# The start addresses of a part of TensorE's operands, moved by 32 to 224 bytes modulo 256

## The chip, the cores and the metric

The kernel runs on one core of one Trainium2 chip. The metric is the device time of one execution in microseconds. The kernel before the change takes 1422.89 us (median of 3 runs, 1422.87 to 1423.13).

## The reference: what is computed

Two kinds of layer alternate, A, B, A, B, each added to its input, on x of 2048 rows (the sequence) by 512 columns in float32:

```python
x = x + _A_ref(_layernorm(x), seq_re, seq_im, hid_re, hid_im)   # a Fourier mixing layer
x = x + _B_ref(_layernorm(x), w1, w2, w3, w4)                   # spatial shift, then an MLP
...                                                             # both once more
```

Layer A is Re(DFT_seq(DFT_hid(x))): two products of x with 512 x 512 matrices and two with 2048 x 2048 matrices. Layer B normalizes, multiplies by w1 (512 x 512), applies gelu, shifts each quarter of the columns by one or two rows up or down, multiplies by w2, adds, normalizes again, multiplies by w3 (512 x 1376), applies gelu, multiplies by w4 (1376 x 512) and adds.

## The kernel before, in words

**Three matmuls for one product.** Every operand of TensorE is split in a high half (rounded to the fp32r format) and a low half (what the rounding left). `mm3` (lines 293 to 296) multiplies high x high (L294), high x low (L295) and low x high (L296) into the same PSUM bank. So nearly every line of the profile for TensorE is L294, L295 or L296, and which product it is shows only in the names of its tiles. A matmul has 128 x 128 weights (the stationary operand, `lh` or `ll`) and a moving operand of 512 columns, or 256 in `first_pair`. There are 6441 of them, beside 12 in float32 on `ident` at the start (L139), which the profile counts as 24. The profile names a matmul's operands as out<-moving,weights.

**Where tiles lie.** One tensor, "arena", holds nearly the whole of SBUF. The tiles lie at hand-written places in it, counted in words of 4 bytes (`at`, `both`; lines 80 to 130), and tiles of different stages share the same places. Sizes and bases are nearly all multiples of 64 words = 256 bytes. So all tiles of TensorE start at one and the same address modulo 256 bytes, except those at and after STG, which starts 32 words past such a multiple: `w11` and one of the two h11 tiles, and the high halves `hr2` to `hr7`, are 128 bytes off the others. Slices of a tile that a matmul reads start at multiples of 128 words within it.

**The stages**, twice (once per layer pair):

- Layer A: `plain_phase` (for the first column block of the first layer), `x_phase` and `y_phase` for each of four blocks of 512 sequence columns. Moving operands are the DFT blocks in the four `ring` tiles: `stream()` hands out the next one, slots 0 to 3 in rotation, each filled by a DMA into a `raw` tile and a split by ACT (L240) and DVE (L257). Weights are the normalized rows and their sums and differences: `ax` (8 tiles, in `x_phase`), `ay` (8 tiles, in `y_phase`; 4 or 2 products per ring tile). Between them `hid` multiplies by the 512 x 512 matrices, with `rr` as weights and ring tiles as moving operand.
- Layer B, first half: `by_pairs` with `shifted` (moving `zt`, two tiles in turn; weights w1) and `mixed` (moving w2; weights `rg`), 16 of each per layer, interleaved.
- Layer B, second half: `prod` (weights `w3b`, moving the blocks `b11` to `b22` and `bt1` to `bt4`, seven products in place of eight, in the manner of Strassen) and `w4_part` (weights `h4`, moving `w4r`, loaded in turn into six or four slots). The last layer has its own code for it: `first_pair` (256 columns; weights `hr` for the high half and `hn` for the low half, moving `un`) and `last_pair` (weights `u1`, `u2` and `w11`).

**What orders the work.** The order is written out by hand; each engine works through its instructions in program order, and semaphores tie them. Hooks (`hook(i)`, `one()`, `at_point`, the slot lists `A` and `D` in `by_pairs`) put the work of ACT, DVE and the DMA queue between the matmuls of TensorE. All DMAs are issued from SyncE's queue. The change touches none of this.

**Names and lines that matter for the change**: `ZW`, `RNG`, `EXT`, `RAWS`, `STG`, `TMP` (lines 70 to 82, the bases of regions: EXT follows the ring and is followed by RAWS, STG and TMP); `ay_at` (L92), `zt` (L95), `turned0` (L99), `ring` (L105), the list of `bt` places (L112), `w4_at` (L119), `w4_in` (L1652), `w4_sum` (L1667).

Of the kernel before, what the change touches and what calls it, by code (L numbers as in the profile page):

```python
# [8 lines left out]
F32 = mybir.dt.float32  # L9
# [4 lines left out]
P = 128  # L14
S, D, F = 2048, 512, 1376
# [4 lines left out]
CH = 512  # L20
NC = S // CH
TC = CH // P
KD = D // P
DH = D // 2
NF = -(-F // P)
# [8 lines left out]
RING = 4  # L34
# [9 lines left out]
def spectral_mlp_kernel(ctx: ExitStack, tc: tile.TileContext, x, ws, hs, w1, w2, w34, out):  # L44
# [26 lines left out]
    ZW = KD * 2 * CH + 32  # L71
    AX, AY = 3 * 2 * DH, 4 * 2 * DH
    W12, XS = 2 * ZW, 2 * ZW + 8 * 2 * CH
    H3 = XS + NT * D
    SPARE = H3 + (LAG + 1) * 2 * CH
    RR = SPARE + 2 * D
    RNG = RR + 2 * KD * 2 * CH
    base = -(-nc.sbuf_base // 32) * 32
    EXT = RNG + RING * 4 * CH
    RAWS = EXT + 6 * D  # L80
    STG = RAWS + RAW * 2 * CH + 32
    TMP = STG + 2 * CH
# [2 lines left out]
    def at(name, word, *shape, dtype=F32R):  # L85
        return nc.alloc_sbuf_tensor_at(name, [P, *shape], dtype, offset=base + 4 * word).ap()

    def both(name, word, *shape):
        return at(name, word, *shape), at(name + "f", word, *shape, dtype=F32)

    tmp = at("tmp", TMP, 6, D, dtype=F32)
    ay_at = (0, AY, H3, H3 + AY, EXT, 2 * AY, 3 * AY, 4 * AY)  # L92
    ay, ayf = zip(*(both(f"ay{k}", ay_at[k], 4, 2, DH) for k in range(NP)))
    ax, axf = zip(*(both(f"ax{k}", XS - 8 * D + k * AX, 3, 2, DH) for k in range(NP)))
    zt, ztf = zip(*(both(f"zt{i}", i * (ZW + 32), KD, 2, CH) for i in range(2)))  # L95
    w12 = [at(f"w12{i}", W12 + i * 4 * CH, 2, 2, CH) for i in range(4)]
    beside = at("beside", XS - 4 * D - 32, 4, D, dtype=F32)
    xs = [at(f"xs{i}", XS + i * 2 * D, 2, D, dtype=F32) for i in range(NP)]
    turned0 = at("turned0", 5 * AY, KD, CH, dtype=F32)  # L99
    turned01 = at("turned01", H3, KD, CH, dtype=F32)  # L100
    spare = at("spare", SPARE, 2, D, dtype=F32)
    (re0, im0), (re1, im1) = ([both(f"rr{i}{h}", RR + (2 * i + h) * 4 * CH, 2, 2, CH) for i in range(2)] for h in range(2))
    rr = [[re0[0], re1[0]], [im0[0], im1[0]]]
    rg = [[at(f"rg{i}{g}", RR + (4 * i + g) * 2 * CH, 2, CH) for g in range(KD)] for i in range(2)]
    ring, ringf = zip(*(both(f"ring{i}", RNG + i * 4 * CH, 2, 2, CH) for i in range(RING)))  # L105
    raw_at = [at(f"raw{i}", RAWS + i * 2 * CH, 2, CH, dtype=F32) for i in range(RAW)]
    raw_at += [at(f"raw{RAW + i}", word, 2, CH, dtype=F32) for i, word in enumerate((EXT + 4 * D, STG))]

    blk, blkf = {}, {}
    for i, word in (("11", H3), ("21", H3 + 4 * CH), ("12", RNG), ("22", RNG + 4 * CH)):  # L110
        blk[i], blkf[i] = both("b" + i, word, 2, 2, CH)
    for i, word in enumerate((0, 4 * CH, RR, RR + 4 * CH)):  # L112
        blk[f"t{i + 1}"], blkf[f"t{i + 1}"] = both(f"bt{i + 1}", word, 2, 2, CH)
    w3b, w3bf = zip(*(both(f"w3b{i}", RNG + 8 * CH + i * 28 * P, 2, 7, 2 * P) for i in range(2)))
    h4 = [at(f"h4{i}", RR + 8 * CH + i * 2 * CH, 2, CH) for i in range(4)]
    hc = at("hc", W12, NF, CH, dtype=F32)
    staged = at("staged", STG, 2, 2, 2 * P, dtype=F32)
    hx = at("hx", STG, 2, CH, dtype=F32)
    w4_at = [2 * ZW + (i - 4) * 2 * CH for i in range(4)] + [W12 + NF * CH + i * 2 * CH for i in range(2)]  # L119
    w4r, w4rf = zip(*(both(f"w4r{i}", word, 2, CH) for i, word in enumerate(w4_at)))  # L120
    scratch = [at(f"scr{i}", RNG + w * 4 * CH, KD, CH, dtype=F32) for i, w in enumerate((2, 3, 0))]
    extra = [at(f"extra{i}", EXT + i * D, D, dtype=F32) for i in range(6)]
    gt = [at(f"gt{g}", RAWS + 4 * D + g * GW, CH + HALO, dtype=F32) for g in range(KD)]
# [1525 lines left out]


    w4_from = [(w34[NF - 1][:, 0], w3e)] + [(w34[f + LAG][:, 1], w4d[f]) for f in range(NF)]
    w4_in = [both(f"w4in{i}", word, 2, CH) for i, word in enumerate((5 * AY, 5 * AY + 2 * CH, STG, EXT + 4 * D))]  # L1652

    def w4_split(i):
        for n in (i - 5, i - 4, i - 3):
# [8 lines left out]
                    nc.sync.dma_start(wf[:, 1], w4_from[n][0])  # L1664

    w4_raw = at("w4raw", STG, 2, CH, dtype=F32)
    w4_sum, w4_sumf = both("w4sum", 5 * AY, 4, 2, 2 * P)  # L1667
    W4_AT = {(0, 2): 0, (0, 3): 1, (1, 1): 2, (1, 2): 3, (1, 3): 4}

    def w4_bring(k):  # L1670
# [261 lines left out]
```

## Time and profile before

| | before |
|---|---|
| median of 3 runs | 1422.89 us |
| the profiled execution | 1423.03 us |
| its span, first to last instruction | 1421.1 us |
| matmul records, weight load records | 6465, 6465 |
| bytes moved by DMA | 306.31 MB |

The page's first part gives the time in which each engine had at least one instruction under way. For TensorE (PE) the matmuls are pipelined: the next one starts long before the last one's modelled end, so the busy time is no measure of how fast they follow each other. That is read from the starts of single matmuls in the timeline, or from the number of matmuls in a window. Busy digits are tenths of a slice of 35.5 us. "PEclk" is the clock that was granted to TensorE.

### The profile page before, as it was taken

How to read it: one execution, taken by the hardware profiler on the slowest of the kernel's cores; microseconds unless marked ns; L12 is line 12 of the kernel's file. 1: busy time of each engine (PE TensorE's matmuls, PEld its weight loads, DVE VectorE, ACT ScalarE, POOL GpSimd, SP SyncE). 2: the span in 40 equal slices, each digit the busy share in tenths (PEclk: the TensorE clock that was granted, in tenths of full speed). 3: DMA queues.
4: the chain of work that ended last, by engine and by line, in shares of the span. 5: the costliest groups of instructions: out<-in, count | busy, mean ns of one | idle time of the engine just before them, and what ended most of it. 6: DMA issues, size and time to landing. Idle time of an engine off the chain costs nothing.

```text
span 1421.1 us, 17861 instructions
## 1 busy us (share of the span) xinstructions
PE 1415.4 (100%) x6465; PEld 1180.1 (83%) x6465; DVE 1187.0 (84%) x1675; ACT 743.0 (52%) x1007; POOL 77.7 (5%) x105
## 2 busy tenths in 40 slices
PE   9999999999999999999999999999999999999998
PEld 7888888888888888888888888888888888899887
DVE  7986998988979888656789989889899788896676
ACT  6663464455566754434555544554555566453351
POOL 2100000000002000000000000000000020000000
PEclk9999999999999999999999999999999999999999
DMA  7867647659754857945556476575696456676864
GB/s 253 279 208 234 210 152 262 193 163 309 238 164 109 294 195 266 354 159 178 196 174 222 152 253 212 158 265 176 193 304 229 134 148 237 202 244 228 311 207 158
DMA packets 136488, 306.31 MB, mean 216 GB/s; under 512 B 9680, under 2 KB 58064, under 8 KB 133712
## 3 DMA queue, kind: packets, MB, share of 16 engines
q1 hardware_dynamic: 136400, 305.17, 65.1%
q8 instruction: 51, 0.84, 0.2%
q14 instruction: 37, 0.30, 0.1%
HBM read 250.87 MB, written 54.26 MB: 215 GB/s over the span
## 4 chain that ended last, share of the span: by engine, by line
PE 93%; DVE 4%; ACT 1%; issue 1%; POOL 0%; DMA 0%; DVEq 0%; ACTq 0%; POOLq 0%
PE psd L294 10%; PE psd L296 10%; PE psd L295 9%; PE psa L296 8%; PE psa L294 8%; PE psa L295 8%; PE psb L296 7%; PE psc L295 7%; PE psc L296 7%; PE psb L294 7%; PE psb L295 7%; PE psc L294 7%; DVE rest L480 0%; ACT tmp L342 0%; DVE ring L257 0%
## 5 line engine op out<-in xcount | busy, mean ns | idle before, releaser
L240 ACT CAST ring<-raw 128x1024 fp32r<-128x1024 f32 x127 | 133.3, 1054 | 78.5 <-PE psd L296 42.9
L257 DVE TENSOR_TENSOR ring<-raw,ring 128x1024 fp32r<-128x1024 f32 x126 | 153.5, 1220 | 13.1 <-ACT ring L240 13.0
L294 PE MATMUL psd<-ring,rr 128*128 128x512 f32 x208 | 80.9, 389 | 0.0
L295 PE MATMUL psd<-ring,rr 128*128 128x512 f32 x208 | 80.9, 389 | 0.0
L296 PE MATMUL psd<-ring,rr 128*128 128x512 f32 x208 | 80.9, 389 | 0.0
L334 POOL TENSOR_TENSOR rs<-ve,mhalf 128x4 f32<-128x4 f32 x16 | 26.9, 1683 | 723.8 <-DVE nm L333 723.8
L247 ACT CAST ring<-ring0f 128x1024 fp32r<-128x1024 f32 x28 | 29.6, 1057 | 50.7 <-DVE ring0f L246 50.7
L257 DVE TENSOR_TENSOR ring<-ring1f,ring 128x512 fp32r<-128x512 f32 (+1 forms) x56 | 53.3, 952 | 0.7 <-ACT ring L243 0.7
L313 POOL TENSOR_TENSOR rs<-ve,mhalf 128x2 f32<-128x2 f32 (+2 forms) x33 | 28.8, 872 | 415.7 <-DVE nb L312 415.7
L342 ACT ACTIVATE tmp<-xs,nb,rs 128x512 f32<-128x512 f32 x56 | 43.5, 814 | 14.6 <-POOL nb L314 14.6
L294 PE MATMUL psc<-ring,ay 128*128 128x512 f32 x128 | 49.8, 389 | 0.0
L295 PE MATMUL psc<-ring,ay 128*128 128x512 f32 x128 | 49.8, 389 | 0.0
L296 PE MATMUL psc<-ring,ay 128*128 128x512 f32 x128 | 49.8, 389 | 0.0
L294 PE MATMUL psb<-ring,ay 128*128 128x512 f32 x128 | 49.8, 389 | 0.0
L295 PE MATMUL psb<-ring,ay 128*128 128x512 f32 x128 | 49.8, 389 | 0.0
L296 PE MATMUL psb<-ring,ay 128*128 128x512 f32 x128 | 49.8, 389 | 0.0
L294 PE MATMUL psa<-ring,ay 128*128 128x512 f32 x126 | 49.0, 389 | 0.0
L295 PE MATMUL psa<-ring,ay 128*128 128x512 f32 x126 | 49.0, 389 | 0.0
L296 PE MATMUL psa<-ring,ay 128*128 128x512 f32 x126 | 49.0, 389 | 0.0
L294 PE MATMUL psd<-ring,ay 128*128 128x512 f32 x126 | 49.0, 389 | 0.0
L295 PE MATMUL psd<-ring,ay 128*128 128x512 f32 x126 | 49.0, 389 | 0.0
L296 PE MATMUL psd<-ring,ay 128*128 128x512 f32 x126 | 49.0, 389 | 0.0
(826 smaller groups left out, 4494.4 us busy)
## 6 DMA issues: line engine op xcount, KB each, us to landing
raw<-in_ws SPq DMA_DIRECT2D x183, 512.0 KB, 5.1
raw<-in_hs SPq DMA_DIRECT2D x56, 512.0 KB, 3.6
w4r<-w4d SPq DMA_DIRECT2D x44, 512.0 KB, 4.5
w3b<-w3d SPq DMA_DIRECT2D x10, 1792.0 KB, 8.9
w3d<-w3b SPq DMA_DIRECT2D x5, 1792.0 KB, 6.9
x1d<-tmp SPq DMA_DIRECT2D x12, 512.0 KB, 6.4
xs<-x1d SPq DMA_DIRECT2D x12, 512.0 KB, 5.0
w4d<-w4in SPq DMA_DIRECT2D x11, 512.0 KB, 4.7
```

Source lines behind the costliest of these rows:

```text
L240: nc.scalar.copy(dest[:, a:b, 0], r[0][:, a:b])
L247: nc.scalar.copy(dest[:, :, 0], lo)
L257: nc.vector.tensor_tensor(lo, src, hi.bitcast(F32), op=ALU.subtract)
L294: nc.tensor.matmul(o, lh, rh, start=first, stop=False, skip_group_check=more)
L295: nc.tensor.matmul(o, lh, rl, start=False, stop=False, skip_group_check=more)
L296: nc.tensor.matmul(o, ll, rh, start=False, stop=last, skip_group_check=more)
L313: nc.gpsimd.tensor_tensor(rs[:, :n], ve[:, :n], mhalf[:, 0, :n], op=ALU.pow)
L334: nc.gpsimd.tensor_tensor(rs, ve, mhalf[:, :, :2], op=ALU.pow)
L342: nc.scalar.activation(o, s, AF.Identity, bias=mr[2], scale=mr[1])
```

## The change

The base of the region EXT moves up by 8 words (32 bytes), and with it everything behind it: RAWS, STG and TMP. Beside this some tiles get offsets of their own. No instruction is added or left out, and the order of the instructions is as before. In words modulo 64 (256 bytes), counted from the level that most tiles keep:

- ring: slots 0 to 2 stay at 0, slot 3 goes to 8
- ay: 0 to 3 stay at 0, ay4 goes to 8 (it lies at EXT), ay5 to 8, ay6 to 16, ay7 to 24
- zt: zt0 to 24, zt1 to 48
- bt: bt1 to 8, bt2 to 40, bt3 and bt4 stay at 0
- w4r: slots 0 to 3 to 56 (8 words lower), slots 4 and 5 stay at 0
- by the shift of EXT: hr0 and hr1, one of the h11 tiles of `first_pair`, both of `last_pair` and a few hn and hs tiles to 8; w11, hr2 to hr7 and the other h11 of `first_pair` from 32 to 40
- ax, rr, rg, w12 (w1 and w2), w3b, h4, b11 to b22, un, u1 and u2 stay at 0
- turned0, w4in and w4sum, which TensorE does not read, move by 24 words with ay7

```diff
-    EXT = RNG + RING * 4 * CH
+    EXT = RNG + RING * 4 * CH + 8
...
-    ay_at = (0, AY, H3, H3 + AY, EXT, 2 * AY, 3 * AY, 4 * AY)
+    ay_at = (0, AY, H3, H3 + AY, EXT, 2 * AY + 8, 3 * AY + 16, 4 * AY + 24)
...
-    zt, ztf = zip(*(both(f"zt{i}", i * (ZW + 32), KD, 2, CH) for i in range(2)))
+    zt, ztf = zip(*(both(f"zt{i}", word, KD, 2, CH) for i, word in enumerate((24, ZW + 16))))
...
-    turned0 = at("turned0", 5 * AY, KD, CH, dtype=F32)
+    turned0 = at("turned0", 5 * AY + 24, KD, CH, dtype=F32)
...
-    ring, ringf = zip(*(both(f"ring{i}", RNG + i * 4 * CH, 2, 2, CH) for i in range(RING)))
+    ring, ringf = zip(*(both(f"ring{i}", RNG + i * 4 * CH + word, 2, 2, CH) for i, word in enumerate((0, 0, 0, 8))))
...
-    for i, word in enumerate((0, 4 * CH, RR, RR + 4 * CH)):
+    for i, word in enumerate((8, 4 * CH + 40, RR, RR + 4 * CH)):
         blk[f"t{i + 1}"], blkf[f"t{i + 1}"] = both(f"bt{i + 1}", word, 2, 2, CH)
...
-    w4_at = [2 * ZW + (i - 4) * 2 * CH for i in range(4)] + [W12 + NF * CH + i * 2 * CH for i in range(2)]
+    w4_at = [2 * ZW + (i - 4) * 2 * CH - 8 for i in range(4)] + [W12 + NF * CH + i * 2 * CH for i in range(2)]
...
-    w4_in = [both(f"w4in{i}", word, 2, CH) for i, word in enumerate((5 * AY, 5 * AY + 2 * CH, STG, EXT + 4 * D))]
+    w4_in = [both(f"w4in{i}", word, 2, CH) for i, word in enumerate((5 * AY + 24, 5 * AY + 24 + 2 * CH, STG, EXT + 4 * D))]
...
-    w4_sum, w4_sumf = both("w4sum", 5 * AY, 4, 2, 2 * P)
+    w4_sum, w4_sumf = both("w4sum", 5 * AY + 24, 4, 2, 2 * P)
```

## The prediction

> Two words are used throughout. A matmul's **distance** is the start address of its weights minus that of its moving operand, modulo 256 bytes; at distance zero the two are **level**, otherwise **apart**. About 0.2% (3 us) is what a measurement of this kernel can tell from no change.
>
> **What bounds the kernel now.** I read the page first, then the waits of TensorE, then its share of a long stretch, then single starts.
>
> ```profile
> PE 1415.4 (100%) x6465; PEld 1180.1 (83%) x6465; DVE 1187.0 (84%) x1675; ACT 743.0 (52%) x1007; POOL 77.7 (5%) x105
> ...
> PEclk9999999999999999999999999999999999999999
> ...
> q1 hardware_dynamic: 136400, 305.17, 65.1%
> ```
>
> PE is busy for the whole span and its clock is never reduced. Busy time of pipelined matmuls says little by itself, so the next view matters more: the waits of TensorE, all of them.
>
> ```profile
> PE psd L139 <- POOL mhalf L55: 1.4, 1, 1.4
> PE psb L426 <- DVE rr L339: 0.2, 1, 0.2
> ```
>
> After the first microseconds TensorE waits for nobody. So the time is the number of matmuls times the interval from one start to the next, and nothing that DVE, ACT or the DMA queue does ends last anywhere. The interval comes from the windows view (PE busy with its count, then the clock) and, more exactly, from the timeline, whose columns are start, duration, engine, line, and operands as out<-moving,weights:
>
> ```profile
> 100.00:1200.00 1100.00, 1099.89 (x4851) 1.00 0.64 212
> ```
>
> ```profile
> 399.71 0.39 PE L294 MATMUL psb<-ring,rr 128*128 128x512 f32 x1
> ...
> 401.97 0.39 PE L295 MATMUL psc<-ring,rr 128*128 128x512 f32 x1
> ```
>
> 1100 us over 4851 matmuls is 0.2268 us, and the ten intervals between the two quoted starts take 2.26 us. The 0.39 us is the pipelined latency of one and is not the price of one. I call 0.2267 us the **settled** interval: nearly all 512-column matmuls keep to it, whatever their tiles, and nearly all of those are level. Only a settled rhythm that can be lost, or bettered, can be moved by this change.
>
> **When the rhythm is lost.** Two places show it at distance zero: a matmul that has a semaphore wait in front of it shifts the start a little, and the following starts need some matmuls to find the rhythm again.
>
> ```profile
> 444.13 0.39 PE L295 MATMUL psd<-w,rg 128*128 128x512 f32 x1
> ...
> 445.52 0.39 PE L295 MATMUL psd<-w,rg 128*128 128x512 f32 x1
> ```
>
> ```profile
> 465.92 0.39 PE L295 MATMUL psd<-w,rg 128*128 128x512 f32 x1
> ...
> 468.24 0.39 PE L296 MATMUL psd<-w,rg 128*128 128x512 f32 x1
> ```
>
> Six intervals take 1.39 us in place of 1.36, and ten take 2.32 in place of 2.267. One loss of the rhythm costs 0.03 to 0.053 us, and it heals after five to ten matmuls.
>
> **The nearest thing to the change in this trace.** The weights w11 of last_pair lie in the staging tile STG, which is 128 bytes off the rest (RAWS ends 32 words past a multiple). So six matmuls in a row are apart by 128, between level ones. The third to eighth rows are those six; the view calls them psa<-h,w.
>
> ```profile
> 1367.51 0.39 PE L295 MATMUL psd<-hs,u 128*128 128x512 f32 x1
> 1367.73 0.40 PE L296 MATMUL psd<-hia,u 128*128 128x512 f32 x1
> 1367.96 0.40 PE L294 MATMUL psa<-h,w 128*128 128x512 f32 x1
> 1368.21 0.40 PE L295 MATMUL psa<-h,w 128*128 128x512 f32 x1
> 1368.44 0.39 PE L296 MATMUL psa<-h,w 128*128 128x512 f32 x1
> 1368.67 0.39 PE L294 MATMUL psa<-h,w 128*128 128x512 f32 x1
> 1368.90 0.39 PE L295 MATMUL psa<-h,w 128*128 128x512 f32 x1
> 1369.13 0.40 PE L296 MATMUL psa<-h,w 128*128 128x512 f32 x1
> 1369.36 0.39 PE L294 MATMUL psa<-hia,u 128*128 128x512 f32 x1
> 1369.59 0.39 PE L295 MATMUL psa<-hs,u 128*128 128x512 f32 x1
> ```
>
> The weights of the next matmul are loaded while the present one streams, so the first interval concerned starts at 1367.73. From there to 1369.59 are eight intervals in 1.86 us; settled ones would take 1.813. Nothing here waits; only the distance changed, and it cost 0.047 us. The first six alone, up to 1369.13, take 1.40 in place of 1.36 us.
>
> The second sample points the other way. In first_pair the matmuls have 256 columns, and their weights, the high halves hr, are either level with the moving tile un (two of the eight hr tiles) or 128 apart (six of them):
>
> ```profile
> 1265.20 0.28 PE L294 MATMUL psd<-un,hr 128*128 128x256 f32 x1
> ...
> 1266.64 0.28 PE L294 MATMUL psb<-un,hr 128*128 128x256 f32 x1
> 1266.76 0.27 PE L295 MATMUL psb<-un,hr 128*128 128x256 f32 x1
> 1266.87 0.28 PE L296 MATMUL psb<-un,hn 128*128 128x256 f32 x1
> ...
> 1268.06 0.28 PE L294 MATMUL psd<-un,hr 128*128 128x256 f32 x1
> ```
>
> The level dozen takes 1.44 us (0.12 each), the dozen with its hr apart 1.42. Here the disturbed rhythm is the faster one, by 0.02 us in twelve, and the shortest single interval is 0.11 in place of 0.12.
>
> **The change part by part.** No instruction is added, removed or reordered; no DMA changes in size or place in the queue, and no wait is added. Only addresses move.
>
> 1. Tiles that TensorE doesn't read (raw, extra, staged and tmp by the shift of EXT; turned0, w4in and w4sum with ay7) move by 32 or 96 bytes. DVE, ACT and the DMA engines touch them, and I cost this at nothing: TensorE has no wait for any of them above, DVE is busy 84%, ACT 52%, the DMA engines 65%. If DVE's accesses became over a tenth slower the cover would be thin; nothing suggests that.
>
> 2. Matmuls that become apart. I walked the matmuls in program order with the diff's offsets. The groups view carries the classes (each line stands for one bank pair and one of the three products):
>
> ```profile
> L294 PE MATMUL psd<-ring,rr 128*128 128x512 f32 x208 | 80.9, 389 | 0.0
> L294 PE MATMUL psc<-ring,ay 128*128 128x512 f32 x128 | 49.8, 389 | 0.0
> L294 PE MATMUL psc<-ring,ax 128*128 128x512 f32 x112 | 43.6, 389 | 0.0
> L294 PE MATMUL psd<-zt,w 128*128 128x512 f32 x64 | 24.9, 389 | 0.0
> L294 PE MATMUL psa<-w4r,h 128*128 128x512 f32 x44 | 17.1, 389 | 0.0
> L294 PE MATMUL psb<-bt,w3b 128*128 128x512 f32 x40 | 15.6, 389 | 0.0
> ```
>
> Of 1536 ring,ay matmuls 864 become apart (ay4 to ay7 against an unmoved ring, and every fourth ring slot); of 960 ring,rr 384; of 1008 ring,ax 96; all 384 of zt,w (64 x 2 bank pairs x 3 products); 444 of 528 w4r,h and all 96 that use w4r as weights; 240 of 480 on bt with w3b; 28 others, 24 of them those of w11, which are apart already. That is 2536 of 512 columns. They come in 180 runs of constant distance (74 of 6, 62 of 12, 22 of 24, 13 of 36, nine others), with 144 level runs between them: 324 runs, each beginning with a change of distance. About nine of these exist already around w11, so 315 are new.
>
> 3. The price of one change of distance is not shown for 32 bytes, only for 128. Bounds: half the w11 excursion, which has two changes, 0.047 / 2 = 0.024 us; and one full loss of rhythm, 0.053 us. The nearest row is the first six intervals of w11: 1.40 against 1.36, 0.037 us before rounding of the starts. I take that: 315 x 0.037 = 11.7 us, with ends 7.4 and 16.7. All of it is on the path, because TensorE is never idle. Below nothing the price could go too, by the 256-column sample; that is a rival.
>
> 4. The 256-column matmuls: the two level hr tiles and hm1 become apart, some ten dozens at 0.02 us saved each: -0.2 us.
>
> A rule of the Trainium skill speaks against any effect. "SBUF — State Buffer", section "Who interferes with whom", has TensorE with two independent read ports, one for the moving operand and one for the weights, and waiting on no one; by it the sum would be zero. The w11 rows do not agree with it, since there only an address differs and 0.047 us appear.
>
> Sum against the profiled execution: 1423.03 + 11.7 - 0.2 = 1434.5 us; the span is 1421.1, with 1.9 us around it. The median of the runs is 1422.89, 0.14 lower, so **1434 us**. With the ends of step 3 the forecast's own range is 1430 to 1440.
>
> **The rivals.**
>
> *Faster: apart is the better state.* If the settled 0.2267 us holds a collision of the weight load with the moving stream, apart operands avoid it. For it: the 256-column dozens. Against it: w11, and every loss of rhythm above, cost time at 512 columns. Priced with 0.02 / 12 = 1.7 ns for each of the 2536: -4.2 us, 1418.6. Priced with the best single interval, 0.11 for 0.12 (112 against 120 ns before rounding): 2536 x 8 ns = -20.3 us, 1402.6. It decides if a run of 12 or more at constant distance settles below 0.2267; w11's six are too few to tell.
>
> The Trainium skill ("TensorE: Matmul & The Clock Gate", section "Wait — 56ns, not 53.3ns?") states 215.7 ns for back-to-back 512-column matmuls at full clock. The settled rows are 11 ns above; were all of that regained, an estimate by that page would be 2536 x 11 ns = 28 us.
>
> *Slower still: apart never settles.* Then each apart matmul pays w11's average, 0.037 / 6 = 6.2 ns: 2536 x 6.2 = 15.7 us, and each of the 144 level runs a loss of 0.03: 4.3. Together 1443.
>
> *No difference.* Distances of 32 to 96 bytes may be too small to matter, and w11's cost may belong to 128 alone: 1423. That the layout isn't what the title says can be excluded for the count above, which follows from the offsets; but half of the matmuls stay level, so a settled interval of 0.2267 will still be seen.
>
> **How the numbers follow.** Forecast (rhythm lost at each change and found again, 1430 to 1440) 0.44; never settles (1440 to 1446) 0.18; no difference 0.11; faster (1402 to 1419) 0.27. Slower by over 0.2% is therefore 0.62, within 0.2% 0.11, faster 0.27. A range that holds 8 in 10 must reach into the faster cases: 1409 to 1444 leaves out the far end of each.
>
> **What would show it.** Right: TensorE still without waits; level runs of rr, ax and rg at 0.2267; the first six intervals after each change of distance near 0.233; the apart count's price in the windows (442 matmuls per 100 us down to about 438). The forecast is wrong if zt,w or w4r,h, which hold one distance for 12 to 36 matmuls, run below 0.2267, if nothing differs, or if a wait of TensorE appears.

## The result and the profile after

The changed kernel takes **1442.3 us** (median of 4 runs, 1442.09 to 1442.33), the kernel before 1422.95 us beside it (4 runs, 1422.87 to 1423.13). The ratio is 1.0135, with a 95% interval of 1.0118 to 1.0153: slower by 19 us. The span of the profiled execution went from 1421.1 to 1440.1 us.

The changed kernel's page, its busy times, granted clock and DMA queue:

```profile
PE 1434.7 (100%) x6465; PEld 1179.9 (82%) x6465; DVE 1188.7 (83%) x1675; ACT 741.1 (51%) x1007; POOL 77.2 (5%) x105
...
PEclk9999999999999999999999999999999999999999
...
q1 hardware_dynamic: 136400, 305.17, 63.5%
```

The same counts of instructions and packets, the same bytes, the full clock. DVE, ACT and POOL are busy for the same time as before to within 2 us; PE's time alone has grown by about as much as the kernel's. The changed kernel's waits of TensorE are one line, the start of the kernel:

```profile
PE psd L139 <- POOL mhalf L55: 1.4, 1, 1.4
```

So no wait was added, and the 19 us must lie in the intervals between matmuls. The windows view of the changed kernel, for the stretch that was shown of before:

```profile
100.00:1200.00 1100.00, 1100.00 (x4778) 1.00 0.62 207
```

4778 matmuls where there were 4851: 0.2302 us each in place of 0.2268. The groups view shows a trace of it in the modelled duration of one matmul (394 ns where 389 stood before, with the same 208 instructions), which is not the price of one:

```profile
L294 PE MATMUL psd<-ring,rr 128*128 128x512 f32 x208 | 81.9, 394 | 0.0
```

Where the intervals grew is seen in the timeline of the changed kernel (start, duration, engine, line, out<-moving,weights). First comes the longest run of one distance, 156 matmuls on w4r, all at 32 bytes (the moving tile starts 224 bytes behind the weights, modulo 256), and then 30 level ones of x_phase:

```profile
697.23 0.40 PE L294 MATMUL psc<-w4r,h 128*128 128x512 f32 x1
...
710.30 0.40 PE L296 MATMUL psa<-w4r,h 128*128 128x512 f32 x1
...
733.40 0.40 PE L296 MATMUL psd<-w4r,h 128*128 128x512 f32 x1
733.64 0.39 PE L294 MATMUL psc<-ring,ax 128*128 128x512 f32 x1
...
735.02 0.39 PE L294 MATMUL psb<-ring,ax 128*128 128x512 f32 x1
...
740.46 0.40 PE L294 MATMUL psa<-ring,ax 128*128 128x512 f32 x1
```

Three readings:

- From 697.23 to 733.64 are 156 intervals in 36.41 us: 0.2334 each. The first 56 (to 710.30) take 13.07, 0.2334; the last 100 take 23.34, 0.2334. Apart matmuls do not find the settled 0.2267 again, however long their run.
- From 733.64 to 735.02 are the first six intervals after the return to level, 1.38 us in place of 1.36.
- From 735.02 to 740.46 are 24 intervals in 5.44 us: 0.2267, settled.

The same holds at another distance. Layer B's first half, zt with w1, at 160 bytes, in the changed kernel's timeline:

```profile
414.70 0.39 PE L294 MATMUL psd<-zt,w 128*128 128x512 f32 x1
414.94 0.39 PE L295 MATMUL psd<-zt,w 128*128 128x512 f32 x1
415.17 0.39 PE L296 MATMUL psd<-zt,w 128*128 128x512 f32 x1
415.40 0.40 PE L294 MATMUL psd<-zt,w 128*128 128x512 f32 x1
...
419.60 0.40 PE L294 MATMUL psd<-zt,w 128*128 128x512 f32 x1
```

21 intervals in 4.90 us, 0.2333; the first three take 0.70 us, which is the same average. The start of the run is no dearer than the rest.

Adding up the intervals of the whole trace gives where the time came from. Each interval is sorted by the tiles that are read in it, as the program has them: the moving tile of the matmul that streams, and the weights of the next one, which are loaded meanwhile.

| intervals | before: count, mean | changed: count, mean | excess over 226.67 ns (120 for 256 columns): before, changed |
|---|---|---|---|
| 512 columns, apart | 25, 232.8 ns | 2543, 233.4 ns | 0.2, 17.1 us |
| 512 columns, level | 5942, 227.0 ns | 3424, 228.1 ns | 2.2, 4.7 us |
| 256 columns | 473, 118.7 ns | 473, 118.0 ns | -0.6, -0.9 us |

16.9 + 2.5 - 0.3 = 19.1 us; 0.2 us less ahead of the first of these matmuls and 0.1 us more behind the start of the last make the 19.0 us by which the span grew. Of the changed kernel's level excess, 3.9 us lie in the first nine intervals after each of the 150 returns to level: 26 ns a return. Against before the level intervals gain less, 2.5 us, because a few long single intervals of before are near the settled price in the changed kernel: at 738.61 us of before, two in a row take 493 and 335 ns, and the same two take 230 and 236 in the changed kernel.

Sorted by distance, the apart intervals of the changed kernel hardly differ: their averages at 32, 64, 96, 128, 160 and 224 bytes are 233.3 to 233.7 ns.

### The profile page after: what moved, and what is told of

It reads as the page before. It is cut to its first block, busy times and chain, and to the rows that moved or that the text cites. A ratio compares the mean times of both kernels' runs of the same rounds, so it can differ in the third digit from the quotient of the medians.

```text
span 1440.1 us, 17858 instructions
## 1 busy us (share of the span) xinstructions
PE 1434.7 (100%) x6465; PEld 1179.9 (82%) x6465; DVE 1188.7 (83%) x1675; ACT 741.1 (51%) x1007; POOL 77.2 (5%) x105
## 4 chain that ended last, share of the span: by engine, by line
PE 99%; DVE 0%; DMA 0%; issue 0%; POOL 0%; DVEq 0%; POOLq 0%
PE psd L294 10%; PE psd L296 10%; PE psd L295 10%; PE psa L294 9%; PE psa L296 9%; PE psa L295 9%; PE psc L294 7%; PE psb L294 7%; PE psc L296 7%; PE psc L295 7%; PE psb L296 7%; PE psb L295 7%; DMA xs<-in_x 0%; PE psd L426 0%; PE psc L426 0%; DVE st L308 0%
```

## The experiments

**The theory** after the result: every 512-column matmul that is apart costs 6.7 ns more, for as long as it is apart, and a return to level costs a little beside this. **The rival** is the forecast's own step: the rhythm is lost at a change of distance and found again within some matmuls, so that the cost goes with the number of changes. Further rivals are that the absolute address matters, or that another engine's moved tiles do.

| kernel | us, median (range) | beside it before | ratio, 95% interval |
|---|---|---|---|
| all_by_32 | 1423.15 (1422.92 to 1423.46) | 1422.99 | 1.0001, 0.9991 to 1.0011 |
| ring_32 | 1446.11 (1445.82 to 1446.33) | 1422.99 | 1.0162, 1.0147 to 1.0177 |
| ring_128 | 1445.03 (1444.36 to 1445.74) | 1422.99 | 1.0155, 1.0139 to 1.017 |
| layer_b_only | 1431.28 (1431.12 to 1431.55) | 1422.99 | 1.0057, 1.004 to 1.0074 |
| level_all | 1423.45 (1422.88 to 1424.08) | 1422.98 | 1.0004, 0.9995 to 1.0012 |
| un_192 | 1422.46 (1422.02 to 1422.59) | 1422.98 | 0.9995, 0.9986 to 1.0005 |
| un_112b | 1420.4 (1419.97 to 1420.86) | 1423.02 | 0.9981, 0.9972 to 0.999 |

Four more (micro, scan, columns, scan_256b) leave the computation out and measure intervals alone, in one execution each.

### all_by_32: the whole arena moved, no distance changed

```diff
-    base = -(-nc.sbuf_base // 32) * 32
+    base = -(-nc.sbuf_base // 32) * 32 + 32
```

> The kernel before with its whole arena moved by 32 bytes: every tile starts elsewhere modulo 256, and every distance is as before. Distance theory (apart matmuls run at 0.2333 us and level ones at 0.2267, whatever the absolute address): no change, 1422.9 +- 0.5. Address theory (the changed kernel lost because tiles, DMA targets included, no longer start at a multiple of 128 bytes): most of the 19 us, 1435 to 1445.

1423.15 against 1422.99 us, a ratio of 1.0001. Moving every absolute address by 32 bytes does nothing, neither for TensorE nor for the tiles of DVE, ACT and the DMA engines. What is left is the place of operands relative to each other.

### ring_32 and ring_128: more apart matmuls, far fewer changes

All four ring tiles move alike, and everything else keeps its distance (the 64 words of padding between zt0 and zt1 go behind the ring to make room; not in the cut below), so the apart matmuls come in few long runs.

```diff
-    ring, ringf = zip(*(both(f"ring{i}", RNG + i * 4 * CH, 2, 2, CH) for i in range(RING)))
+    ring, ringf = zip(*(both(f"ring{i}", RNG + i * 4 * CH + 8, 2, 2, CH) for i in range(RING)))   # ring_128: + 32
```

> All four ring tiles 32 bytes on, everything else level as before: 3504 matmuls of layer A are apart by 32 bytes, in a handful of long runs, so there are hardly any changes of distance. Theory that an apart run never settles (6.67 ns for each apart matmul): 3504 x 6.67 ns = 23.4 us, 1446. Theory of the forecast (a price per change of distance, then settled): about ten changes x 0.037 us, 1423.3. Theory that the address of DMA targets is what costs: little, since only the ring moves, below 1425.

> The same with 128 bytes. If every distance but zero costs the same: 1446, and single intervals that average 0.2333 us. If the price depends on the distance (128 being half of 256): another time than with 32 bytes by more than 2 us. Per change of distance: 1423.3.

The windows views, first of ring_32, then of ring_128:

```profile
100.00:1200.00 1100.00, 1100.00 (x4761) 1.00 0.62 206
```

```profile
100.00:1200.00 1100.00, 1100.00 (x4767) 1.00 0.62 207
```

Fewer matmuls fit in than in the changed kernel (4778), though there is hardly a change of distance: in the whole of ring_32 the apart matmuls stand in one run of 1776, one of 1728 and the four of six on w11 that before has too. ring_32 takes 1446.11 us where the theory says 1446 and the rival 1423.3: the rival has fallen, since the excess of 23 us is that of 3504 matmuls (6.6 ns each) and not of a dozen changes. Without the first few at the start of the kernel, the 512-column apart intervals average 233.33 ns in ring_32 and 232.86 in ring_128, so a distance of 128 bytes is hardly better than one of 224 (the ring is the moving operand and moved up by 32).

### layer_b_only: a part of the change alone

The changed kernel with ring, ay and EXT put back; zt, bt and w4r stay moved.

```diff
-    EXT = RNG + RING * 4 * CH + 8
+    EXT = RNG + RING * 4 * CH
...
-    ay_at = (0, AY, H3, H3 + AY, EXT, 2 * AY + 8, 3 * AY + 16, 4 * AY + 24)
+    ay_at = (0, AY, H3, H3 + AY, EXT, 2 * AY, 3 * AY, 4 * AY)
...
-    ring, ringf = zip(*(both(f"ring{i}", RNG + i * 4 * CH + word, 2, 2, CH) for i, word in enumerate((0, 0, 0, 8))))
+    ring, ringf = zip(*(both(f"ring{i}", RNG + i * 4 * CH + word, 2, 2, CH) for i, word in enumerate((0, 0, 0, 0))))
```

> The changed kernel with layer A undone: ring, ay and EXT back at level, so that only zt, bt and w4r (layer B) keep their offsets. 1164 matmuls of 512 columns become apart, by 32 to 224 bytes, in 65 to 70 short runs (6 to 156 matmuls). Never-settles theory: 1164 x 6.67 = 7.8 us, and some 27 ns for each of about 60 returns to level, 1.6 us: 1432.3. Per-change theory of the forecast: some 130 changes x 0.037 = 4.8 us: 1427.7.

1431.28 us: 8.3 above before, and 1164 x 6.67 ns = 7.8 us of it are the apart matmuls' price. That is 1.0 below the theory's number and 3.6 above the rival's. The returns to level cost what the theory had put on them: in the trace the first nine intervals after the 64 returns hold 1.7 us above the settled price, 26 ns a return. The theory's number is too high because it left the rest as it was: the other level intervals hold 0.8 us above the settled price, where the same ones hold 1.7 in before.

### micro and scan: the interval by itself

In micro and scan one tile of weights and one moving tile lie in an SBUF that nobody else touches, and the moving operand starts d words behind the weights, so that the distance of the prediction is 256 bytes less 4d. Loads and stores of x, copies that fill the two tiles, and runs of 6 to 48 matmuls are all there is.

```python
for d in range(64):                                # scan; micro: some d, other widths, bf16
    triples(5, CH, LEVEL, (d, d, d))               # 30 matmuls of 512 columns
    triples(1, CH, LEVEL, LEVEL)
for d in range(64):
    triples(5, 256, LEVEL, (d, d, d))              # 30 of 256 columns
```

> A kernel that leaves the whole computation out: 2600 matmuls in a row on two constant tiles, with nothing running beside them; the output is a copy of x and of PSUM. Runs of 36 at one distance each (4 to 252 bytes, 512 columns) between level runs of 24; then 256 and 384 columns; then triples with one operand apart; then bf16. If it is the distance alone: level 0.2267 us, all distances from 32 to 224 at 0.2333 in the mean, without any DMA, ACT or DVE work beside. If other engines' accesses matter: all at the level figure. For 4 to 28 bytes no theory has a number; for the mixed triples the forecast's view (each change costs) gives over 0.2333, the never-settles view about 0.2289 (one of three apart). For 256 columns the trace of the changed kernel gives 0.120 level and 0.118 apart. In bf16 open.

> The computation left out again: 30 matmuls at each of the 64 distances of whole words, first with 512 columns (6 level ones between two distances), then with 256 (none between). The moving operand starts 4, 8, ... 252 bytes behind the level. If level is the best there is at 512 columns, none of the 63 others is below 0.2267 us; the coarse scan had 0.2289 at 64 bytes and 0.2317 at 16 as the next best. At 256 columns the coarse scan had 0.1133 at 192 bytes against 0.1200 level and 0.118 at the others; a neighbourhood of low values around 192 would make it a window, a single one a resonance. If the collision of the weight load with the stream were what level operands suffer from, as the faster rival of the prediction has it, many distances at 512 columns should be near 0.218.

The timeline joins equal instructions: first start, time from the first start to the last end, and the count. So the interval is the time less one matmul's duration (0.39 us at 512 columns, 0.40 at the slowest, 0.28 at 256), divided by the count less one. Rows of scan: level, 32 bytes, 68 bytes (one of the slowest), then 256 columns, level and 112 bytes. They stand in order of time, so level comes first, 68 bytes third:

```profile
33.25 5.15 PE L72 MATMUL ps<-mv,wt 128*128 128x512 f32 x22
...
100.14 5.29 PE L72 MATMUL ps<-mv,wt 128*128 128x512 f32 x22
...
175.28 5.20 PE L72 MATMUL ps<-mv,wt 128*128 128x512 f32 x21
...
568.35 2.80 PE L72 MATMUL ps<-mv,wt 128*128 128x256 f32 x22
...
668.30 2.56 PE L72 MATMUL ps<-mv,wt 128*128 128x256 f32 x21
```

(5.15 - 0.39) / 21 = 0.2267, (5.29 - 0.39) / 21 = 0.2333, (5.20 - 0.40) / 20 = 0.2400; at 256 columns (2.80 - 0.28) / 21 = 0.120 and (2.56 - 0.28) / 20 = 0.114 us. No DVE or ACT instruction and no load or store of data runs beside these, so the effect is TensorE's own: its two operands against each other. Of the 64 distances level is the fastest for 512 columns (226.67 ns; the next ones about 228.9, at seven distances; 12 lie above 236.6). The six distances of the change are all among the dearer ones (232.8 to 234.1); a moving operand 64 bytes behind its weights, which the change does not have, costs 228.9 in micro and scan, so the expectation that all distances from 32 to 224 cost 0.2333 was wrong there.

For 256 columns level is not the best: it takes 120.0 ns, and four distances (16, 112, 144 and 192 bytes of d) take 113.3 to 113.9, but the dearest take about 123. So the outcome of the faster rival of the prediction holds for some distances at 256 columns and for none at 512. With 384 columns micro has 173.3 ns level and 32 bytes apart, and 175.8 at 128 bytes.

Micro also has triples in which one of the three matmuls is apart. Never settling alone would give 228.9 ns, a price per change over 233.3. The ten kinds average 229.1 to 233.7, 231.1 in the mean: where the distance changes at every third matmul, going in and out costs about as much again as the apart matmul itself, so neither view has it alone.

In micro the same weights and moving tiles, in bf16, rows of d = 0 and d = 128 bytes:

```profile
601.71 4.48 PE L90 MATMUL ps<-mb,wb 128*128 128x512 bf16 x20
...
625.67 4.70 PE L90 MATMUL ps<-mb,wb 128*128 128x512 bf16 x21
```

(4.48 - 0.38) / 19 = 0.2158 us and (4.70 - 0.38) / 20 = 0.2160: in bf16 the four distances tried (0, 32, 64 and 128 bytes) do not differ.

### columns: is it the weight load that collides?

Weights of 128, 96, 64 and 32 columns, so that the load is shorter (its records last 188, 161, 134 and 108 ns) while the moving stream stays as it is. The computation is left out.

```python
for cols in (128, 96, 64, 32):
    for d in (0, 8, 17, 32):
        some(d, cols, CH, 5)                       # weights wt[:, a : a + cols], 30 matmuls
    some(0, cols, CH, 2)
```

> The computation left out: runs of 30 matmuls on constant tiles with 128, 96, 64 and 32 columns of weights at distances 0, 32, 68 and 128 bytes, 512 columns of moving operand; then 256 columns at 0, 32 and 192 bytes. If the weight load's reads collide with the stream, the excess over 512 / 2.4 = 213.3 ns shrinks with the columns of the weights: apart by 68 bytes from 26.7 ns (128 columns) to about 13 (64) and 7 (32), and the level one from 13.3 likewise. If the excess belongs to where the moving operand starts, alone, it is the same for all numbers of weight columns.

Rows of columns, 96 columns level and at 128 bytes, then 32 columns level and at 68 bytes:

```profile
63.88 4.53 PE L103 MATMUL ps<-mv,wt 128*96 128x512 f32 x19
...
84.85 4.70 PE L103 MATMUL ps<-mv,wt 128*96 128x512 f32 x20
...
125.05 4.56 PE L103 MATMUL ps<-mv,wt 128*32 128x512 f32 x19
...
139.03 4.93 PE L103 MATMUL ps<-mv,wt 128*32 128x512 f32 x20
```

With these shorter loads the duration of one matmul is again near 0.39 us, so 18 intervals take 4.14 (0.230), 19 take 4.31 (0.227), 18 take 4.17 (0.232), 19 take 4.53 (0.238). With 32 columns the slowest distance still costs 238 ns, and level has become slower, 232; with 96 columns 128 bytes is the best distance, and level is not. So the excess does not shrink with the load: that the weight load delays the stream in proportion to its length has fallen, and so has the other expectation, that the place of the moving operand alone matters. At 256 columns the number of weight columns counts as well, and again not in proportion: level takes 120.0 ns with 128 weight columns and 113.3 with 64 or 32, but 192 bytes take 113.3, 119.0 and 113.3. What remains is that the interval depends on the distance and on the shape of both operands together.

### level_all and un_192: the apart matmuls of before undone

level_all brings the kernel before wholly level: w11, hr2 to hr7 and the other tiles that lay 128 bytes off. un_192 is the same with un moved, so that all 468 matmuls of first_pair have one distance, for which micro and scan gave 113.3 ns. To make room, both also put `ident` into the arena and move padding; these lines are not in the cut.

```diff
-    STG = RAWS + RAW * 2 * CH + 32
+    STG = RAWS + RAW * 2 * CH + 64
...
-        units = [at(f"un{i}", RNG + 8 * CH + 28 * P + i * 2 * W, 2, W) for i in range(7)]
+        units = [at(f"un{i}", RNG + 8 * CH + 28 * P + 48 + i * 2 * W, 2, W) for i in range(7)]   # un_192 only
```

> The same with un level: all matmuls of the kernel level. By the scans the 468 then run at 0.1200: 56.2 us, 0.6 more than before; w11 gives back 0.2: 1423.3. If level is best at 256 columns as it is at 512, below 1422.9.

> The kernel before with every 512-column matmul level (w11 too, by 64 words of padding in place of 32 ahead of STG) and the moving tiles un of the 468 matmuls with 256 columns 192 bytes behind both halves of their weights. By the two scans those run at 0.1133 us: 468 x 0.1133 = 53.0 us in place of the 55.6 that they take before, and w11 gives back 4 x 0.047: together -2.7, 1420.2 us. If a rhythm found on idle tiles does not hold beside DVE, ACT and DMA work, 1422 to 1424.

The timeline of level_all and that of un_192, 20 intervals each:

```profile
1264.31 0.28 PE L294 MATMUL psd<-un,hr 128*128 128x256 f32 x1
...
1266.71 0.28 PE L296 MATMUL psa<-un,hn 128*128 128x256 f32 x1
```

```profile
1264.15 0.28 PE L294 MATMUL psd<-un,hr 128*128 128x256 f32 x1
...
1266.51 0.28 PE L296 MATMUL psa<-un,hn 128*128 128x256 f32 x1
```

level_all holds 0.120 as expected, and its 1423.45 us cannot be told from before either. un_192 was a miss: 2.36 / 20 = 0.118 us in place of 0.1133, from the first matmul to the last in a nearly unbroken pattern (118, 117, 118, 118 ns ...). Its 1422.46 us cannot be told from before.

### scan_256b and un_112b: is 256 columns a matter of order too?

scan_256b runs first_pair's own order of operands at 256 columns, in two passes with different predecessors; the computation is left out.

```python
for d in range(0, 64, 2):
    for u in range(3):
        unit(u, d)                                 # 12 matmuls, as first_pair's multiply()
    unit(0, 0)
for d in range(64, 0, -1):
    for u in range(3):
        unit(u, d % 64)
```

> The computation left out. The matmuls of 256 columns in first_pair's own pattern (four row blocks, the two moving halves 256 words apart, high weights twice, then low weights), 36 at each distance, first at the even distances with 12 level ones between, then at all 64 in descending order. Un_192 ran at 0.1178 us where the earlier scans had 0.1133 at the same distance. If the halves' own places are the reason, 192 bytes gives 0.1178 here too, in both passes, and another distance may give 0.1133 in both. If the waits and neighbours of the real kernel broke the rhythm, 192 bytes gives 0.1133 here. If the rhythm depends on where the run before it ended, the two passes differ.

The timeline of scan_256b at 16 bytes, first and second pass:

```profile
40.84 3.37 PE L93 MATMUL ps<-mv,wt 128*128 128x256 f32 x27
...
470.33 3.34 PE L93 MATMUL ps<-mv,wt 128*128 128x256 f32 x28
```

(3.37 - 0.28) / 26 = 0.119 and (3.34 - 0.28) / 27 = 0.113 us: at 16 bytes the two passes differ, so the rhythm depends on what ran before. At 112 they agree (113.6 and 113.6 ns), at 192 too (113.4 and 113.3). At 144 bytes, for which scan gave 113.3, both passes take 118.7. un_112b is un_192 with 28 words in place of 48.

```diff
-        units = [at(f"un{i}", RNG + 8 * CH + 28 * P + i * 2 * W, 2, W) for i in range(7)]
+        un = at("un", RNG + 8 * CH + 28 * P, 7 * 2 * W + 64)
+        units = [un[:, 28 + i * 2 * W:28 + (i + 1) * 2 * W].rearrange("p (a w) -> p a w", a=2) for i in range(7)]
```

> The kernel before with all TensorE operands level, except that in first_pair the moving tile un starts 112 bytes behind its weights (modulo 256), for the 468 matmuls of 256 columns. The scans with idle other engines gave 113.6 ns for this distance in both passes, 120.0 level. If the distance alone decides, the 468 take 53.2 us in place of 55.6 and the kernel 1420.6 us (before 1422.95). If the interval depends on what went before, as un_192 showed with 117.8 ns in place of 113.3, they take 55.1 us or more and the kernel stays between 1422.3 and 1423.5.

The timeline and one group of un_112b:

```profile
1264.04 0.28 PE L294 MATMUL psd<-un,hr 128*128 128x256 f32 x1
...
1266.31 0.28 PE L296 MATMUL psa<-un,hn 128*128 128x256 f32 x1
```

```profile
L294 PE MATMUL psb<-un,hr 128*128 128x256 f32 x50 | 13.8, 275 | 0.0
```

20 intervals in 2.27 us, 0.1135; over all 468 the mean is 113.41 ns, 53.1 us where before takes 55.6. The kernel takes 1420.4 us, 2.6 below before, ratio 0.9981 (0.9972 to 0.999): faster than both kernels, with un 112 bytes off and everything else level. By the traces, 2.5 of the 2.6 us are those of the 468.

## Why the prediction was right in sign and short in size

- **What bounds the kernel**: right. No wait appeared, the clock stayed, and the time is the sum of TensorE's intervals, before and after.
- **Step 1** (tiles that TensorE does not read): right. all_by_32 moves all of them at 1.0001, and the waits of the changed kernel name none.
- **Step 2** (which matmuls become apart): right. The program's 2536 apart matmuls give 2543 apart intervals in the trace, 25 of which before has too.
- **Step 3** (the price of one change): this step failed. It took the apart run to heal like a level one, and so 315 changes at 0.037 us, 11.7 in all. The excess is 19.4 us in place of it, 0.062 per change and beyond the step's upper end of 0.053. The price is on the matmul: 2518 newly apart intervals x 6.7 ns = 16.9 us. ring_32 shows it best: 23 us with two long apart runs. What heals is the return to level, at 26 ns each, 3.9 us in all, of which 2.5 are left against before. The healing had been read from two places at level (444.13 and 465.92 us; that a wait causes these was not tested) and carried over to distances where no run of before is longer than six matmuls. The w11 rows held the right price, 0.037 us over six intervals, but were read as the price of a change.
- **Step 4** (256 columns): right in sign, -0.3 us measured, -0.2 forecast.
- **The Trainium skill** ("SBUF — State Buffer", section "Who interferes with whom") gives TensorE two independent read ports, and by it the sum was zero. Measured: 233.3 against 226.7 ns in scan, where no other engine works. For fp32r operands the measurement decides against a sum of zero; the bf16 rows, with no difference between four distances, agree with the rule.
- **Slower still: apart never settles** is what happened: 1443 forecast, 1442.3 measured. Its terms were 15.7 and 4.3 us; they came out at 16.9 and 3.9, and the long intervals of before that are gone took off the difference. It had a chance of 0.18, against 0.44 for the forecast.
- **Faster: apart is the better state**: fell for 512 columns. The run that was to decide it, 12 or more matmuls at constant distance, stays at 0.2333 (zt,w and w4r,h). For some distances at 256 columns apart is better, as the dozens of before hinted: un_112b gains 2.6 us with it. Why was not shown; the collision that the rival supposed is not confirmed by that.
- **No difference**: fell, and with it the thought that 32 bytes are too little to matter: 32 costs as much as 128.
- The range of 1409 to 1444 held the time only because it reached into this slower rival; the forecast's own, 1430 to 1440, did not. Of the signs named ahead, the windows count was to go from 442 per 100 us to 438; by the rows shown it went from 441 to 434.

What would have helped ahead of time: the w11 rows fit "0.024 us per change" and "6.2 ns per matmul" equally well, and the two sums, 7.4 and 15.7 us, lie far apart. The text chose the change because nearby losses of rhythm heal, and those were losses at distance zero.

## What to carry to other kernels

For a TensorE-bound kernel in fp32r, treat the start of the weights minus the start of the moving operand, modulo 256 bytes, as a tuning parameter: 512-column matmuls with 128 weight columns ran fastest level, 256-column ones at a distance that has to be tried in the kernel itself. A small excess seen in a short run of matmuls can be a cost of entry or a cost of each; price both, and look for a longer run, or make one, before choosing. When TensorE has no waits left, the number of matmuls in a window shows such an effect at once, while the busy shares show nothing.

## What the runs showed of the hardware that was not expected

- The interval of fp32r matmuls depends on the distance of the operands, with the SBUF otherwise quiet: 226.67 ns level, 228.75 to 240.0 at the other 63 distances of scan (512 columns, 128 weight columns). At 512 columns the averages of micro and scan agree to within 0.7 ns, and about a quarter of them are whole multiples of 6.67 ns: 226.67, 233.33 and 240.0.
- In bf16 there is no such effect: 215.8 ns at d = 0, 32, 64 and 128 bytes. The Trainium skill ("TensorE: Matmul & The Clock Gate", section "Wait — 56ns, not 53.3ns?") states 215.7 ns; the bf16 rows agree, the fp32r ones, 226.67 at best, do not.
- The best distance changes with the shape: at 512 columns with 96 weight columns it was 128 bytes of the four tried (226.7 ns), with 128 columns level.
- At 256 columns the rhythm can depend on what went before: 118.7 or 113.3 ns at 16 bytes in scan_256b's two passes. In un_192 it is 117.8 where the scans gave 113.3.

**What stays open.** What in the hardware makes the interval depend on the distance was not shown; a collision in proportion to the weight load is excluded by columns, and nothing here measures the ports themselves. Why un_192 stays in the pattern of 117.8 ns while un_112b finds 113.4 was not tried further; the kernel's waits, the matmuls ahead of first_pair and the traffic of DVE, ACT and the DMA engines differ from the scans', and none of them was taken away alone.
